# A two-branch attention kernel: state accumulated chunk by chunk in PSUM, weights resident early, four-head score groups, TensorE in written order

## The chip, the cores and the metric

The kernel runs on one core of one Trainium2 chip. The metric is the device time of one execution in microseconds (us), and lower is better. The kernel before took 442.96 us, the median of six executions (442.25 to 444.06). Every later comparison is against runs of the kernel before on the same chip in the same session; there its median lay between 443.7 and 447.4 us.

## The reference, cut to what matters

The input `x` has 2048 rows of 640 features. Two branches of 32 heads with 20 features each are computed from it and mixed with a gate for each row.

```python
def _A_ref(x, wqkv, w_phi, wo):                 # branch A: linear attention, not causal
    q, k, v = ...                               # [B, H, S, 20] from x @ wqkv
    pq, pk = q @ w_phi, k @ w_phi               # a 20x20 matrix for each head
    phi_q = concat([softmax(pq), softmax(-pq)])
    phi_k = concat([softmax(pk), softmax(-pk)])
    kv = einsum('bhsf,bhsd->bhfd', phi_k, v)    # the key-value state, over all rows
    z  = einsum('bhsf->bhf', phi_k)
    num = einsum('bhqf,bhfd->bhqd', phi_q, kv)
    den = einsum('bhqf,bhf->bhq', phi_q, z) + 1e-6
    return (num / den).reshape(B, S, D) @ wo

def _B_ref(x, wq, wk, wv, wo, beta):            # branch B: four segments of 512 rows
    phi = lambda t: where(t > 0, t + 1.0, exp(t))
    for s in range(4):
        p = softmax(qs @ ks.T * scale + mask)   # causal within the segment
        a_dot = p @ vs
        a_mem = (phi(qs) @ M) / (phi(qs) @ z + 1e-6)   # memory of earlier segments
        outs.append(g * a_mem + (1 - g) * a_dot)       # g = sigmoid(beta), one per head
        M = M + phi(ks).T @ vs
        z = z + sum(phi(ks))
    return concat(outs) @ wo

g = sigmoid((x * gate_w).sum(-1))
return g * _A_ref(x, ...) + (1 - g) * _B_ref(x, ...)
```

Of the kernel before, what the change touches and what calls it, by code (L numbers as in the profile page):

```python
# [8 lines left out]
ALU = mybir.AluOpType  # L9
# [6 lines left out]
def kernel(  # L16
# [36 lines left out]

    const = ctx.enter_context(tc.tile_pool(name="const", bufs=1))
    psw = ctx.enter_context(tc.tile_pool(name="psw", bufs=4, space=PSUM))
    pst = ctx.enter_context(tc.tile_pool(name="pst", bufs=2, space=PSUM))
# [6 lines left out]
    def stile(name):  # L63
        return pst.tile([P, 2, 512], F32, name=name, tag="st")

    xT = const.tile([P, KC, S], BF16, name="xT")
    apool_stack = ExitStack()
    apool = apool_stack.enter_context(tc.tile_pool(name="apool", bufs=1, side="right"))
    a0_stack = ExitStack()
    a0 = a0_stack.enter_context(tc.tile_pool(name="a0", bufs=1, side="right"))  # L70

    xv = x2.rearrange("(c p) d -> p c d", p=P)
    x_nat = a0.tile([P, NCH, D], BF16, name="x_nat")
    wnat_k = a0.tile([P, KC, D], BF16, name="wnat_k")
    wnat_q = a0.tile([P, KC, D], BF16, name="wnat_q")
    Wc = a0.tile([P, NG6, DH], BF16, name="Wc")
    WvA = apool.tile([P, KC, D + 1], BF16, name="WvA")
    nc.sync.dma_start(out=x_nat[:, 0:4, :], in_=xv[:, 0:4, :])
    nc.scalar.dma_start(out=wnat_k, in_=A_wqkv[:, D:2 * D].rearrange("(c p) n -> p c n", p=P))
    nc.sync.dma_start(out=WvA[:, :, 0:D],  # L80
                      in_=A_wqkv[:, 2 * D:3 * D].rearrange("(c p) n -> p c n", p=P))
    wphi_rows = A_w_phi.rearrange("h f g -> (h f) g")
    nc.gpsimd.memset(Wc[:, NG6 - 1, :], 0.0)
# [3 lines left out]
    nc.sync.dma_start(out=WvA[:, :, D:D + 1],  # L87
                      in_=gate_w.rearrange("(c p o) -> p c o", p=P, o=1))
    beta_b = const.tile([P, H], BF16, name="beta_b")
    nc.scalar.dma_start(out=beta_b, in_=B_beta.partition_broadcast(P))  # L90
    nc.sync.dma_start(out=x_nat[:, 4:8, :], in_=xv[:, 4:8, :])
    nc.scalar.dma_start(out=x_nat[:, 8:12, :], in_=xv[:, 8:12, :])
    nc.sync.dma_start(out=x_nat[:, 12:16, :], in_=xv[:, 12:16, :])
    nc.scalar.dma_start(out=wnat_q, in_=A_wqkv[:, 0:D].rearrange("(c p) n -> p c n", p=P))
# [9 lines left out]
    def block_mask(name, n, step, width, parts):  # L104
# [10 lines left out]
    chk4 = block_mask("chk4", 4, 32, 32, P)  # L115
    ind = const.tile([P, 4], BF16, name="ind")
    nc.vector.tensor_copy(out=ind, in_=chk4)

    Wphi = a0.tile([P, NG6, 6, DH], BF16, name="Wphi")
    nc.vector.tensor_tensor(out=Wphi[0:120],  # L120
                            in0=Wc[0:120, :, None, :].to_broadcast([120, NG6, 6, DH]),
                            in1=m6[0:120, None, :, None].to_broadcast([120, NG6, 6, DH]),
                            op=ALU.mult)
# [3 lines left out]

    def fold_weight(wn, dst, nm):
        WT = a0.tile([P, NG6, KC, P], BF16, name=f"WT{nm}")
        for g in range(NG6):  # L130
            gw = GW[g]
            tp = wtile("wtp", BF16)
            for ic in range(KC):
                nc.tensor.transpose(out=tp[0:gw, ic * P:(ic + 1) * P],
                                    in_=wn[:, ic, g * 120:g * 120 + gw], identity=ident_b)
            if g % 2 == 0:
                nc.scalar.copy(out=WT[0:gw, g], in_=tp[0:gw, 0:D].rearrange("p (c k) -> p c k", k=P))
            else:
                nc.vector.tensor_copy(out=WT[0:gw, g],
                                      in_=tp[0:gw, 0:D].rearrange("p (c k) -> p c k", k=P))  # L140
        for ic in range(KC):
            for (g0, g1) in ((0, 4), (4, 6)):
                ps = wtile("wfold")
                for g in range(g0, g1):
                    gw = GW[g]
                    o = (g - g0) * 120
                    nc.tensor.matmul(ps[:, o:o + gw], lhsT=WT[0:gw, g, ic, :],
                                     rhs=Wphi[0:gw, g].rearrange("p h f -> p (h f)")[:, 0:gw],
                                     start=True, stop=True)
                w = sum(GW[g0:g1])  # L150
                if g0 == 0:
                    nc.scalar.copy(out=dst[:, ic, 0:w], in_=ps[:, 0:w])
                else:
                    nc.vector.tensor_copy(out=dst[:, ic, 480:480 + w], in_=ps[:, 0:w])

    def x_transpose(sc):
        tp = wtile("xtp", BF16)
        for c in range(KC):
            nc.tensor.transpose(out=tp[:, c * P:(c + 1) * P], in_=x_nat[:, sc, c * P:(c + 1) * P],
                                identity=ident_b)  # L160
        nc.vector.tensor_copy(out=xT[:, :, sc * P:(sc + 1) * P],
                              in_=tp[:, 0:D].rearrange("p (c k) -> p c k", k=P))

    EkN = apool.tile([P, NCH, EKW], BF16, name="EkN")
    nc.gpsimd.memset(EkN[:, :, 1280:EKW], 0.0)
    vA = apool.tile([P, NCH, D], BF16, name="vA")
    gl = const.tile([P, NCH], F32, name="gl")
    KVZ = const.tile([P, 2, NG6, 6, 22], BF16, name="KVZ")
    nc.vector.tensor_copy(
        out=KVZ[:, :, :, :, DH].rearrange("p s g h -> p (s g) h"),  # L170
        in_=m6[:, None, :].to_broadcast([P, 2 * NG6, 6]))
    zc = apool.tile([P, 2 * NG6, 64], BF16, name="zc")
    zh = apool.tile([P, 2 * NG6, 2], BF16, name="zh")
    zf = apool.tile([P, 2 * NG6], BF16, name="zf")

    with tc.tile_pool(name="a1w", bufs=3, side="right") as a1w:
        def mm_x(ps, sc, W, lo, hi):
            for c in range(KC):
                nc.tensor.matmul(ps, lhsT=xT[:, c, sc * P:(sc + 1) * P], rhs=W[:, c, lo:hi],  # L179
                                 start=(c == 0), stop=(c == KC - 1))  # L180

        def a1_v(sc):
            for hf in range(2):
                ps = wtile("va_ps")
                w = 320 + hf
                mm_x(ps[:, 0:w], sc, WvA, 320 * hf, 320 * hf + w)
                nc.scalar.copy(out=vA[:, sc, 320 * hf:320 * hf + 320], in_=ps[:, 0:320])
                if hf:
                    nc.vector.tensor_copy(out=gl[:, sc:sc + 1], in_=ps[:, 320:321])

        def a1_k(sc):
            ps = stile("ka_ps")
            for hf in range(2):
                mm_x(ps[:, hf, 0:320], sc, WkA, 320 * hf, 320 * hf + 320)
            Ek = a1w.tile([P, 2, D], BF16, name="Ek")
            for sgn in range(2):
                nc.scalar.activation(out=Ek[:, sgn].rearrange("p (t f) -> p t f", t=2),  # L197
                                     in_=ps[:, :, 0:320], func=ACT.Exp,
                                     scale=1.0 if sgn == 0 else -1.0)
            ksum = a1w.tile([P, 2 * H], F32, name="ksum")  # L200
            krec = a1w.tile([P, 2 * H], F32, name="krec")
            for sgn in range(2):
                nc.vector.tensor_reduce(out=ksum[:, sgn * H:(sgn + 1) * H],  # L203
                                        in_=Ek[:, sgn].rearrange("p (h f) -> p h f", f=DH),
                                        axis=AX.X, op=ALU.add)
            nc.vector.reciprocal(out=krec, in_=ksum)  # L206
            nc.gpsimd.tensor_tensor(  # L207
                out=EkN[:, sc, 0:1280].rearrange("p (h f) -> p h f", f=DH),
                in0=Ek.rearrange("p s (h f) -> p (s h) f", f=DH),
                in1=krec[:, :, None].to_broadcast([P, 2 * H, DH]), op=ALU.mult)  # L210

        for sc in range(4):
            x_transpose(sc)
        fold_weight(wnat_k, WkA, "k")
        for sc in range(NCH):
            a1_v(sc)
            a1_k(sc)
            if sc + 4 < NCH:
                x_transpose(sc + 4)
        fold_weight(wnat_q, WqA, "q")  # L220
    a0_stack.close()

    gS = const.tile([P, NCH], F32, name="gS")
    omgS = const.tile([P, NCH], F32, name="omgS")
    nc.scalar.activation(out=gS, in_=gl, func=ACT.Exp, scale=-1.0)
    nc.vector.tensor_scalar_add(out=gS, in0=gS, scalar1=1.0)
    nc.vector.reciprocal(out=gS, in_=gS)
# [325 lines left out]
    for u in fill_bkv(0):  # L553
        u()
# [98 lines left out]
```

## The kernel before: the parts that the change touches

The kernel has three stages. The first part projects keys and values of branch A and builds its state. Attention then walks through 4 segments times 8 groups of four heads. A tail writes out the last segment.

In the first part, all 16 chunks of rows are projected first. The state follows as twelve passes over all chunks. A GpSimd chain sums `zh`, and only then are the weights of branch B loaded.

```python
    for sgn in range(2):
        for g in range(NG6):
            ps = wtile("kv_ps")
            for sc in range(NCH):
                lhsT = EkN[:, sc, sgn * D + g * 120:sgn * D + g * 120 + P]
                nc.tensor.matmul(ps[:, 0:gw], lhsT=lhsT, rhs=vA[:, sc, g * 120:g * 120 + gw],
                                 start=(sc == 0), stop=(sc == NCH - 1), ...)
                nc.tensor.matmul(ps[:, 128 + 4 * sc:132 + 4 * sc], lhsT=lhsT, rhs=ind, ...)
            ...
    for j in range(1, 32):
        nc.gpsimd.tensor_tensor(out=zh, in0=zh, in1=zcv[:, :, :, j], op=ALU.add)
    ...                                         # only now: weights of branch B
    nc.sync.dma_start(out=WkB, in_=B_wk...)     # and WvB, WoA, WoB
    for c in range(KC):
        nc.sync.dma_start(out=wq_st, in_=B_wq[c * P:(c + 1) * P, :])
        nc.gpsimd.tensor_copy(out=WqB[:, c, :, 0:DH], in_=wq_st...)
```

PSUM holds four work buffers (`wtile`) and two score buffers (`stile`) of twice that size. Almost everything in attention takes a work buffer and gives it back when the last reader has finished:

```python
    def wtile(name, dt=F32):                    # psw has bufs=4
        return psw.tile([P, 512], F32, name=name, tag="w")
    def stile(name):                            # pst has bufs=2
        return pst.tile([P, 2, 512], F32, name=name, tag="st")

    def b_q(s, g):                              # query projection of a group
        ps = wtile("qb_ps")
        ...                                     # 5 matmuls of 512 columns
        nc.vector.tensor_copy(out=qT, in_=ps)
        if s > 0:
            nc.scalar.activation(out=eq, in_=ps, func=ACT.Exp)    # second reader of ps
            ...

    def b_v(s, c):                              # value projection of a chunk
        for hf in range(2):
            ps = wtile("vb_ps")
            mm_x2(ps[:, 0:320], 4 * s + c, WvB, ...)
            nc.scalar.copy(out=vb[...], in_=ps[:, 0:320]...)

    def b_qk(qT, kT, PTs, cs):                  # scores, one pair of heads at a time
        for pr in range(2):
            st = stile("st_ps")
            for c in cs:
                for i in range(2):
                    nc.tensor.matmul(st[:, i, o:o + n], ..., tile_position=(64 * pr + 32 * i, 0))
            nc.scalar.activation(out=PTs[pr]..., in_=st[:, :, 0:w], func=ACT.Exp, scale=SCALE_B)

    def a3_num(s, qc, half):                    # a "num unit": output of branch A, 1/8 of a segment
        for sgn in range(2):
            ps = wtile("num_ps")                # two work buffers
            ...                                 # 3 matmuls
            nc.scalar.copy(out=dz[...], in_=v[:, :, DH:DH + 2])
        ...                                     # VectorE: xx, rr, 1/rr, cs (four small steps)
        for sgn in range(2):                    # only this frees the two buffers
            nc.vector.tensor_tensor(out=ts[:, sgn, ...], in0=pss[sgn][:, :, 0:DH],
                                    in1=cs[...], op=ALU.mult)
```

Beside the groups' own work, each segment has "filler" units in a queue: key and value projections of the next segment (`kb`, `vb`), the `pq` and `num` units of branch A, and the output projection of the segment before. The loop emits a share of them after each third of a group. The first query projection of the next segment comes after everything else:

```python
            mix = []                            # a3 = 6 pq units, then 8 num units
            while fins or a3:
                if a3: mix.append(a3.pop(0))
                if fins: mix.append(fins.pop(0))
            for t in range(max(nm, nr)):        # rest = kb, vb of the next segment
                if t < nr: queue.append(rest[t])
                if t < nm: queue.append(mix[t])
        for t, cs in enumerate(((0,), (1, 3), (2,))):
            b_qk(qT, kT, PTs, cs)
            ...                                 # next group's b_q, b_kT, unless a new segment
            want = (ntot * sl) // nslots
            while done < want:
                queue[done]()
                done += 1
        if k + 1 < NG and (k + 1) % G == 0:     # new segment: query comes last
            nxt = (b_q(s1, g1), b_kT(s1, g1))
```

The order in the code is not the order on TensorE. In the kernel before, a scheduler reorders the instructions of every engine when the program is built, and may put a later, independent matmul ahead of a waiting one.

The softmax here doesn't subtract the row's maximum and nothing guards it: scores larger than these inputs give would overflow.

## Time and profile before

| | before |
|---|---|
| median (first six executions) | 442.96 us |
| profiled span | 443.1 us |
| first query projection (`qb`) starts | 121.9 us |
| attention (to the end of the last value matmul) | 301.6 us |
| tail | 19.6 us |

The first view gives windows of the profile of the kernel before, one for each stage and one for the end of a segment. The columns are the window and its length in us, then the busy time of TensorE (PE), its weight load, VectorE (DVE), ScalarE (ACT) and GpSimd (POOL), each with a count of instructions. Then come the granted TensorE clock, the share of DMA and GB/s.

```profile
core 0: us, PE busy (x) PEld busy (x) DVE busy (x) ACT busy (x) POOL busy (x), PEclk, DMA share, GB/s
0.00:23.40 23.40, 9.70 (x86) 8.28 (x87) 6.57 (x19) 6.13 (x10) 3.47 (x18) 1.00 0.93 297
23.40:121.90 98.50, 81.33 (x900) 63.51 (x899) 58.19 (x117) 45.32 (x101) 58.47 (x64) 0.88 0.08 24
121.90:423.50 301.60, 278.85 (x3184) 161.82 (x3182) 195.12 (x582) 224.65 (x394) 150.65 (x319) 0.93 0.02 8
423.50:443.10 19.60, 14.31 (x128) 9.94 (x124) 4.72 (x12) 3.41 (x8) 0.86 (x1) 1.00 0.12 43
180.00:190.00 10.00, 7.07 (x73) 3.96 (x72) 8.78 (x27) 3.63 (x9) 5.19 (x11) 0.56 0.01 2
```

In attention TensorE is busy for 278.9 of 301.6 us, so it is idle for only 22.8. No other engine comes near it over the whole stage. The last row shows why an average is not enough. In these 10 us, around the end of the first segment, VectorE is at 88%, ScalarE has hardly anything to do, and TensorE's clock averages 0.56.

The second view is the list of TensorE's waits over the whole kernel before, with the total in us, the number of waits and the longest.

```profile
engine line waited for: us in total, times, longest us
PE vb_ps L312 <- ACT ek L326: 12.3, 1, 12.3
...
```

The 12.3 us wait is the one between the first part and attention. The `ek` step was itself held up by the late `WqB` copies on GpSimd (12.7 us of ScalarE's idle time before `ek` ended on them).

The third view gives groups of TensorE instructions in attention: busy us, mean ns of one, then the idle time just before them and what ended it.

```profile
L383 PE MATMUL st_ps<-qT,kT 32*128 32x384 bf16 (+3 forms) x512 | 64.0, 312 | 9.2 <-ACT PT_5667 L388 0.8 <-ACT PT_4163 L388 0.8 <-ACT PT_3949 L388 0.6
...
L475 PE MATMUL num_ps<-KVZ,Eq 128*128 128x132 bf16 (+1 forms) x192 | 21.2, 230 | 4.5 <-DVE ts L495 1.4 <-DVE td L435 1.3 <-DVE kT L369 0.6
```

Another view is TensorE's timeline in the kernel before, where the second segment begins. Each line has start and length in us, the line of code, what was written and read, how many, and in brackets the idle time before and what ended it.

```profile
185.94 2.31 PE L347 MATMUL qb_ps<-xT,WqB 128*128 128x512 bf16 x5 [0.85 <-DVE ts L495]
...
190.59 0.40 PE L383 MATMUL st_ps<-qT,kT 32*128 32x512 bf16 x4
```

The first query projection of the segment waits for a work buffer that `ts` frees, and the segment's first scores follow 4.7 us later. This is one of the bubbles that the change sets out to remove.

### The profile page before, as it was taken

What the parts mean: (1) busy time and instruction counts of PE and PEld (TensorE: products, weight loads), DVE (VectorE), ACT (ScalarE), POOL (GpSimd) and SP (SyncE); (2) the same over time, 40 slices, a digit from 0 to 9 for tenths busy, and PEclk for the clock granted to TensorE, in tenths of its full rate; (3) what the DMA queues carried; (4) which work ended last, traced back from release to release, by engine and by line L of the source; (5) the groups of instructions that cost most, each with busy time, mean ns of one, the idle gap of its engine ahead of it and who ended that gap; (6) DMA issues with size and microseconds to landing.
All of it is one profiled execution on the core that took longest, in us unless ns stands there. A gap on an engine that the chain in (4) does not pass through costs nothing.

```text
span 443.1 us, 10565 instructions
## 1 busy us (share of the span) xinstructions
PE 384.2 (87%) x4288; PEld 243.6 (55%) x4288; DVE 264.6 (60%) x728; ACT 279.5 (63%) x511; POOL 213.4 (48%) x402
## 2 busy tenths in 40 slices
PE   2599996991799999789998979999989899989996
PEld 2477775890545554446554555555555546555564
DVE  0468989321453467866547887444588764587731
ACT  1266675210479987477786665876774699785711
POOL 3037776817234547634335554443455645565710
PEclk9999999696799999599998899999898999896899
DMA  7950000000100000000000000000000000000001
GB/s 246 341 201 1 3 0 1 2 3 15 31 0 2 2 1 1 2 1 2 0 17 1 16 17 16 1 1 1 18 16 1 31 1 17 1 17 1 16 31 44
DMA packets 11240, 12.49 MB, mean 28 GB/s; under 512 B 1977, under 2 KB 11193, under 8 KB 11193
## 3 DMA queue, kind: packets, MB, share of 16 engines
q1 hardware_dynamic: 9209, 9.53, 6.6%
q10 hardware_dynamic: 1984, 2.30, 1.5%
q8 instruction: 33, 0.54, 0.5%
q14 instruction: 14, 0.11, 0.1%
HBM read 9.21 MB, written 2.62 MB: 27 GB/s over the span
## 4 chain that ended last, share of the span: by engine, by line
PE 58%; DVE 15%; ACT 14%; issue 5%; POOL 4%; DMA 3%; POOLq 0%; DVEq 0%; ACTq 0%
PE o_ps L525 8%; PE st_ps L383 7%; PE qb_ps L347 6%; PE nd_ps L402 5%; PE pq_ps L457 5%; PE ka_ps L179 4%; PE va_ps L179 4%; PE vb_ps L312 4%; PE kv_ps L250 3%; PE kb_ps L312 3%; DMA Wc<-in_A_w_phi_dram 3%; DVE ts L495 2%; PE num_ps L475 2%; DVE xx L484 2%; POOL zh L262 2%
## 5 line engine op out<-in xcount | busy, mean ns | idle before, releaser
L383 PE MATMUL st_ps<-qT,kT 32*128 32x384 bf16 (+3 forms) x512 | 64.0, 312 | 9.2 <-ACT PT_5667 L388 0.8
L207 POOL TENSOR_TENSOR EkN<-Ek,krec 128x1280 bf16<-128x1280 bf16 x16 | 37.7, 2355 | 36.4 <-DVE krec L206 36.0
L347 PE MATMUL qb_ps<-xT,WqB 128*128 128x512 bf16 x160 | 44.8, 410 | 1.7 <-DVE ts L495 1.6
L312 PEld LDWEIGHTS <-xT 128*128 128x128 bf16 x320 | 30.6, 100 | 28.5 <-issue 16.0
L383 PEld LDWEIGHTS <-kT 32*128 32x128 bf16 x512 | 19.1, 92 | 38.5 <-issue 28.4
L529 ACT CAST osb<-o_ps 128x320 bf16<-128x320 f32 x32 | 13.7, 429 | 40.4 <-PE o_ps L525 40.3
L351 DVE CAST qT<-qb_ps 128x512 bf16<-128x512 f32 x32 | 22.0, 688 | 27.3 <-PE qb_ps L347 27.2
L179 PEld LDWEIGHTS <-xT 128*128 128x128 bf16 x320 | 30.7, 98 | 11.4
L312 PE MATMUL vb_ps<-WvB,xT 128*128 128x320 bf16 x160 | 25.8, 310 | 12.3 <-ACT ek L326 12.3
L500 POOL TENSOR_TENSOR oA<-ts 128x360 bf16<-128x360 f32 (+1 forms) x32 | 27.5, 860 | 18.3 <-DVE ts L495 17.1
L431 DVE RECIPROCAL rd<-nd_ps 128x16 f32<-128x16 f32 x32 | 8.1, 253 | 46.0 <-PE nd_ps L402 45.9
L457 PE MATMUL pq_ps<-xT,WqA 128*128 128x512 bf16 x120 | 30.1, 379 | 0.3 <-DVE kT L369 0.2
L495 DVE TENSOR_TENSOR ts<-num_ps,cs 128x360 f32<-128x360 f32 (+1 forms) x64 | 28.4, 484 | 2.0
L197 ACT ACTIVATE Ek<-ka_ps 128x640 bf16<-128x640 f32 x32 | 20.8, 701 | 13.9 <-PE ka_ps L179 13.0
L203 DVE TENSOR_REDUCE ksum<-Ek 128x32 f32<-128x640 bf16 x32 | 24.7, 814 | 2.1 <-ACT Ek L197 1.8
L347 PEld LDWEIGHTS <-WqB 128*128 128x128 bf16 x160 | 14.1, 102 | 21.6 <-issue 9.1
L312 PE MATMUL kb_ps<-WkB,xT 128*128 128x320 bf16 x160 | 25.4, 303 | 0.3 <-DVE kT L369 0.3
L445 POOL TENSOR_TENSOR oB<-td,tm 128x320 bf16<-128x320 f32 x24 | 20.6, 859 | 10.5 <-DVE td L435 10.1
L475 PE MATMUL num_ps<-KVZ,Eq 128*128 128x132 bf16 (+1 forms) x192 | 21.2, 230 | 4.5 <-DVE ts L495 1.4
L179 PE MATMUL ka_ps<-WkA,xT 128*128 128x320 bf16 x160 | 24.9, 299 | 0.0
L179 PE MATMUL va_ps<-WvA,xT 128*128 128x320 bf16 (+1 forms) x160 | 24.5, 300 | 0.0
L326 ACT ACTIVATE ek<-kb_ps 128x320 bf16<-128x320 f32 x24 | 10.1, 443 | 19.7 <-POOL WqB L307 12.7
(470 smaller groups left out, 1018.6 us busy)
## 6 DMA issues: line engine op xcount, KB each, us to landing
out_dram<-osb SPq DMA_DIRECT2D x16, 160.0 KB, 1.8
x_nat<-in_A_x_dram SPq DMA_DIRECT2D x3, 640.0 KB, 7.6
wnat_k<-in_A_wqkv_dram ACTq DMA_DIRECT2D x1, 800.0 KB, 7.8
WvA<-in_A_wqkv_dram SPq DMA_DIRECT2D x1, 800.0 KB, 10.6
wnat_q<-in_A_wqkv_dram ACTq DMA_DIRECT2D x1, 800.0 KB, 13.3
WkB<-in_B_wk_dram SPq DMA_DIRECT2D x1, 800.0 KB, 9.5
WvB<-in_B_wv_dram SPq DMA_DIRECT2D x1, 800.0 KB, 10.4
WoA<-in_A_wo_dram SPq DMA_DIRECT2D x1, 800.0 KB, 10.9
```

Source lines behind the costliest of these rows:

```text
L179: nc.tensor.matmul(ps, lhsT=xT[:, c, sc * P:(sc + 1) * P], rhs=W[:, c, lo:hi], start=(c == 0), stop=(c == KC - 1))
L203: nc.vector.tensor_reduce(out=ksum[:, sgn * H:(sgn + 1) * H], in_=Ek[:, sgn].rearrange("p (h f) -> p h f", f=DH), axis=AX.X, op=ALU.add)
L207: nc.gpsimd.tensor_tensor(out=EkN[:, sc, 0:1280].rearrange("p (h f) -> p h f", f=DH), in0=Ek.rearrange("p s (h f) -> p (s h) f", f=DH), in ...
L312: nc.tensor.matmul(ps, lhsT=xT[:, c, sc * P:(sc + 1) * P], rhs=W[:, c, lo:hi], start=(c == 0), stop=(c == KC - 1))
L347: nc.tensor.matmul(ps, lhsT=WqB[:, c, 4 * g:4 * g + 4, :], rhs=xT[:, c, s * L:(s + 1) * L], start=(c == 0), stop=(c == KC - 1))
L383: nc.tensor.matmul(st[:, i, o:o + n], lhsT=kT[r:r + 32, c * P:(c + 1) * P], rhs=qT[r:r + 32, c * P:L], start=True, stop=True, tile_positio ...
L402: nc.tensor.matmul(nd[:, j * 84 + i * V1:j * 84 + (i + 1) * V1], lhsT=PTs[i // 2][:, i % 2, o:o + P], rhs=vb[:, c, 4 * g + i, :], start=(j ...
L457: nc.tensor.matmul(ps, lhsT=WqA[:, c, g * 120:g * 120 + P], rhs=xT[:, c, s * L:(s + 1) * L], start=(c == 0), stop=(c == KC - 1))
L475: nc.tensor.matmul(ps[:, o:o + GH[g] * 22], lhsT=segs[s].Eq[g][:, sgn, qc * P:(qc + 1) * P], rhs=KVZ[:, sgn, g, 0:GH[g], :].rearrange("p h ...
L495: nc.vector.tensor_tensor(out=ts[:, sgn, 0:nh, :], in0=pss[sgn][:, :, 0:DH], in1=cs[:, sgn, 0:nh, None].to_broadcast([P, nh, DH]), op=ALU. ...
L500: nc.gpsimd.tensor_tensor(out=segs[s].oA[:, qc, h0 * DH:(h0 + nh) * DH].rearrange("p (h d) -> p h d", d=DH), in0=ts[:, 0, 0:nh, :], in1=ts ...
L525: nc.tensor.matmul(ps[:, 0:320], lhsT=segs[s].oT[X][:, k5 * P:(k5 + 1) * P], rhs=Wo[:, k5, hf * 320:hf * 320 + 320], start=(n == 0), stop= ...
```

## The change

The change has five intents.

1. Small loads go first, and all weights of branch B are loaded at the start and kept.
2. The state is accumulated in PSUM after each chunk, between the projections, and not in passes at the end. The `WqB` copies go to VectorE.
3. The score matmuls of all four heads of a group are issued together. The 24 value copies of attention go from ScalarE to VectorE (the copies of the first segment's values move too).
4. The filler units are dealt by an estimated TensorE time for each, beginning with projections. The next segment's first query is issued a group ahead.
5. TensorE keeps the written order (`manual_schedule`); the other engines are still reordered.

The core of the diff (cuts marked with "..."; remarks after `#` are added here):

```diff
+    ctx.enter_context(tc.manual_schedule(engines={mybir.EngineType.PE}))
...                                             # loads: small ones first, all weights here
+    wload(WkB, B_wk)
+    wload(WvB, B_wv)
...
+    nc.gpsimd.memset(WqB[:, :, :, DH:32], 0.0) # fills of branch B's buffers, now at the start
+        nc.gpsimd.memset(kp[:, :, :, DH:32], 0.0)
+        nc.gpsimd.memset(pk[:, :, :, DH:32], 0.0)
...
+    def a1_kv(sc):                             # state matmuls of one chunk
+        for idx in (0, 1, 2, 3, 4, 6, 7, 8, 9, 10, 5, 11):
+            nc.tensor.matmul(acc[bank][:, o:o + gw], lhsT=lhsT,
+                             rhs=chunk[sc].v[:, g * 120:g * 120 + gw],
+                             start=(sc == 0 and o == 0), stop=(sc == NCH - 1), ...)
...
+    for sc in range(NCH):
+        if sc + 2 < NCH:
+            a1_v(sc + 2)
+        a1_k(sc)
...
+        if sc >= 2:
+            a1_kv(sc - 2)
+    for c in range(KC):
+        nc.vector.tensor_copy(out=WqB[:, c, :, 0:DH], ...)
-    for sgn in range(2):                       # the twelve passes of the state
-        for g in range(NG6):
...
-            nc.scalar.copy(out=vb[:, c, hf * 16:hf * 16 + 16, 0:DH],
+            nc.vector.tensor_copy(out=vb[:, c, hf * 16:hf * 16 + 16, 0:DH],
...
     def b_qk(qT, kT, PTs, cs):
+        st2 = [pst.tile([P, 2, 512], F32, name="st_ps", tag="st") for _ in range(2)]
+        for c in cs:
+            for i in range(4):
+                nc.tensor.matmul(st2[i // 2][:, i % 2, o:o + n], ..., tile_position=(32 * i, 0))
...
+            base = deal(fill_bkv(s + 1) if s + 1 < NSEG else [], fill_a3(s))
+            head = []
+            while base and sum(t for t, _ in head) < total / G - own + 0.5:
+                head.append(base.pop(0))
+            queue = head + deal(base, fins)
...
             if t == 0 and k + 1 < NG:
-                s1, g1 = divmod(k + 1, G)
-                if not (g1 == 0):
-                    nxt = (b_q(s1, g1), b_kT(s1, g1))
+                nq = b_q(*divmod(k + 1, G))    # the next segment's first query too
...
-        if k + 1 < NG and (k + 1) % G == 0:
-            nxt = (b_q(s1, g1), b_kT(s1, g1))
```

The `deal` order is worked out in the code, so it can be read off. In the two middle segments, the number of `num` units in each of the eight groups was 0 0 0 0 2 2 3 1 before, and is 0 0 0 0 0 2 2 4 after.

## The prediction

> **What bounds it now.** The windows view splits the 442.96 us into four stages.
> 1. 0 to 23 us, loading. TensorE is busy 9.7 us; the chain of waits begins with the 23 KB load `Wc`, 12.5 us to landing behind large loads.
> 2. 23 to 122 us, first part. Projections are TensorE-dense until 69.5. Then the query fold (69.5 to 80.4, 6.0 us busy), 384 state matmuls (16 us), and about 13 us idle: the waits view has TensorE 12.3 us behind ScalarE `ek`, which waits for GpSimd's `WqB` copies, queued behind its 32-step `zh` chain and late weight loads.
> 3. 122 to 423.5 us, attention. Busy: TensorE 279, ScalarE 225, VectorE 195, GpSimd 151 of 301.5. At full-clock spacing (216 ns for 512 columns, 136 for 320, 25 for 21) TensorE needs about 225. Limits alternate: VectorE is 84 to 90% busy at segment ends, where the `num` units bunch, and ScalarE is then starved (3.6 of 10 us in 180 to 190), because the next segment's first query projection comes last.
> 4. 423.5 to 443, output tail.
>
> The clock records hold about 65 us at exactly half clock, in multiples of 3.41 us, 41 of them in attention. [...]
>
> **What the change does on the critical path.**
> - Loading: small loads first, gate weights as a row plus one transpose. Steady projections begin near 17 instead of 23: -6.
> - State chunk by chunk: the same 384 matmuls (78 ns a pair, 0.94 us a chunk), between projections. Per chunk TensorE needs about 4.2 us against ScalarE 2.9, VectorE 2.8, GpSimd 3.4 (2.36 for `EkN`, four adds of 0.24): still TensorE-bound. The fold's bubbles go: -5.
> - Weights early, `WqB` on VectorE, no `zh` tail: -13. Given back: about 4, as VectorE waits for `wq_st` and ScalarE for `beta_b`, landing at 20 to 36 us.
> - So attention begins near 96 instead of 122.
> - Attention: same work, except 24 value copies (10 us) moving from ScalarE to VectorE. Laying the written unit order over traced durations, the busiest engine of each group sums to about 257 us after, 252 before: `num` units bunch even more tightly into a segment's last quarter. No gain from balance. The gain is the next segment's first query issued a group ahead, removing three boundary bubbles (4 to 6 each), and less half clock: 301 becomes about 280.
> - Four-head score groups: four 512-column score matmuls already took 0.33 us when issued together[...]. Only split pairs gain: under 4, mostly off the path.
> - Tail unchanged, 19 to 20.
>
> **Prediction: 96 + 280 + 19 = 395 us**, 80% range 374 to 415. Faster by over 2%: 0.95; within 2%: 0.04; slower: 0.01.
>
> **What would show it.** First `qb` matmul at 90 to 102; no TensorE wait over 4 us after 20 us; state matmuls spread over 25 to 90 us; mean granted clock at least 0.95; VectorE busy about 205 us in attention, over 85% in a segment's last two groups; ScalarE without the boundary dips; attention lasting 265 to 297.
>
> **What would make it wrong.** Written order leaves TensorE standing where the scheduler had other work: score matmuls now need both score buffers free, and `num` units hold buffers while VectorE is behind. Then attention stays at 300, the total near 415. Or VectorE keeps up better than its traced durations suggest: attention 260, total 375. Early loads could starve `x` and delay the first part.

Two of the numbers can be set against the traces. Four 512-column score matmuls issued together took 0.39 to 0.40 us in the kernel before, not 0.33. "20 to 36 us" was an estimate; in the kernel after VectorE's copies of `wq_st` start between 27.7 and 35.3 us, and `beta_b` is read at 35.5.

## The result, and the profile after

The kernel after took 439.75 us (median of 20 runs, 438.17 to 444.61), against 443.72 us for 40 runs of the kernel before. The ratio of fast runs is 0.992, with a 95% interval of 0.989 to 0.994. It is the same within 2%, far from the predicted 395. A ratio here is the mean time of one kernel's fast runs over that of the other's fast runs of the same rounds, so it is not quite the ratio of the medians quoted. Executions over 1.5% slower than the fastest of the same kernel are left out of the means.

| stage | before | predicted | after | change |
|---|---|---|---|---|
| loading and first part | 121.9 | 96 | 98.9 | -23.0 |
| attention | 301.6 | 280 | 316.6 | +15.0 |
| tail | 19.6 | 19 | 22.3 | +2.7 |
| profiled span | 443.1 | 395 | 437.8 | -5.3 |

The windows of the kernel after, cut as before at the first query projection and at the end of attention:

```profile
0.00:21.90 21.90, 11.88 (x101) 8.91 (x101) 10.37 (x19) 7.00 (x13) 11.17 (x26) 1.00 0.95 309
21.90:98.90 77.00, 74.16 (x885) 57.94 (x886) 57.29 (x105) 45.84 (x128) 54.76 (x84) 1.00 0.11 33
98.90:415.50 316.60, 265.12 (x3187) 155.87 (x3185) 206.38 (x608) 217.69 (x369) 149.24 (x318) 0.92 0.02 8
415.50:437.80 22.30, 16.52 (x126) 10.96 (x122) 4.79 (x13) 3.41 (x8) 1.74 (x3) 0.85 0.09 30
250.00:260.00 10.00, 5.54 (x38) 2.69 (x35) 9.36 (x25) 3.98 (x11) 5.04 (x9) 0.76 0.06 19
```

The first part did what it was meant to do: between 21.9 and 98.9 us TensorE is busy for 74.2 of 77.0 us at full clock. Attention gave most of that back. TensorE's busy time there fell by 13.7 us, but its idle time rose from 22.8 to 51.5. The last row is again the end of a segment, this time the second. VectorE is at 94%, TensorE at 55%, and ScalarE is starved just as before.

The groups of TensorE instructions in attention, after:

```profile
L426 PE MATMUL st_ps<-qT,kT 32*128 32x128 bf16 (+3 forms) x512 | 44.4, 315 | 12.0 <-ACT PT_2021 L434 0.9 <-ACT PT_2287 L434 0.9 <-DVE kT L413 0.9
...
L518 PE MATMUL num_ps<-KVZ,Eq 128*128 128x132 bf16 (+1 forms) x192 | 19.1, 226 | 16.7 <-DVE ts L538 8.4 <-DVE td L481 2.5 <-ACT eq L399 2.0
```

The idle time before `num` went from 4.5 to 16.7 us, half of it behind `ts`, the VectorE step that frees a `num` unit's two work buffers.

The list of TensorE's waits in attention, after:

```profile
PE num_ps L518 <- DVE ts L538: 8.4, 7, 1.8
PE mz_ps L465 <- DVE ts L538: 3.8, 4, 1.0
...
PE vb_ps L231 <- ACT eq L399: 2.4, 4, 0.8
PE kT_ps L410 <- DVE ts L538: 2.2, 2, 1.2
```

Most of these waits end on two releasers: `ts` on VectorE, and `eq` on ScalarE. The latter is the second reader of a query projection's work buffer. Neither of the two is an input of `mz` or `kT`. What those matmuls need from them is the buffer.

The following timeline shows TensorE in the kernel after at the end of the second segment, with the columns as above. Its first line is the third segment's first query projection, now a group ahead.

```profile
241.81 1.25 PE L391 MATMUL qb_ps<-xT,WqB 128*128 128x512 bf16 x5
...
249.76 0.62 PE L518 MATMUL num_ps<-KVZ,Eq 128*128 128x132 bf16 x9
251.23 0.35 PE L518 MATMUL num_ps<-KVZ,Eq 128*128 128x132 bf16 x3 [0.85 <-DVE td L481]
253.34 0.67 PE L518 MATMUL num_ps<-KVZ,Eq 128*128 128x132 bf16 x6 [1.77 <-DVE ts L538]
253.94 0.39 PE L426 MATMUL st_ps<-qT,kT 32*128 32x512 bf16 x4
255.27 2.31 PE L391 MATMUL qb_ps<-xT,WqB 128*128 128x512 bf16 x5 [0.93 <-DVE ts L538]
...
258.73 0.46 PE L465 MATMUL mz_ps<-vB_158,phik_157 128*128 128x84 bf16 x4 [0.86 <-DVE ts L538]
```

And VectorE in the same stretch of the kernel after:

```profile
252.84 0.81 DVE L538 TENSOR_TENSOR ts<-num_ps,cs 128x280 f32<-128x280 f32 x2
...
254.68 0.97 DVE L538 TENSOR_TENSOR ts<-num_ps,cs 128x360 f32<-128x360 f32 x2
...
258.23 0.79 DVE L538 TENSOR_TENSOR ts<-num_ps,cs 128x280 f32<-128x280 f32 x2
```

Read the two together. The `num` matmuls belong to three units in a row (six matmuls each), and each unit takes two of the four work buffers. VectorE's records show 2.6 to 3.5 us for the chain of one unit, from `xx` to `ts`. So the third unit waits for the first unit's `ts` (253.34, in the course of the one from 252.84). The third segment's first scores (253.94) stand behind it, though their query had been projected by 243.06. Then the query projection of that segment's second group waits for the second unit's `ts` (255.27), and behind it `mz` waits for the third unit's (258.73). In this stretch no matmul overtakes a waiting one: the scores start 0.6 us after the wait of 1.77 us has ended. The query projection then takes 2.31 us for five matmuls, because half clock has set in (granted clock 0.50 from 255.3 to 262.1). At full clock (241.81) the same five take 1.25 us.

The following table is worked out from the starts of the groups' first score matmuls. It sums groups 6 and 7 of a segment and group 0 of the next, over the three boundaries:

| | groups 6, 7 and next 0, three boundaries |
|---|---|
| before | 94.1 us |
| after | 108.3 us |

The difference, 14.2 us, is nearly all of attention's +15.0. So the net loss sits at the ends of the segments. The runs below split this. With the units in the order of before (e1) the sum is 95.0 us, but with TensorE free and the units still dealt (e2) it stays at 109.1. What the free order gains in e2 lies in the other groups: up to the last group's first scores they take 183.8 us there, against 193.4 in the kernel after and 195.1 in the kernel before.

### The profile page after: what moved, and what is told of

The parts are those of the page before. It is cut to its first block, busy times and chain, and to the rows that moved or that the text cites. A ratio compares the mean times of both kernels' runs of the same rounds, so it can differ in the third digit from the quotient of the medians.

```text
span 437.8 us, 10636 instructions
## 1 busy us (share of the span) xinstructions
PE 367.7 (84%) x4289; PEld 233.7 (53%) x4289; DVE 278.8 (64%) x743; ACT 273.9 (63%) x515; POOL 216.9 (50%) x430
## 4 chain that ended last, share of the span: by engine, by line
PE 56%; DVE 18%; ACT 16%; issue 5%; POOL 3%; DMA 2%; SPq 0%; POOLq 0%; DVEq 0%; ACTq 0%
PE o_ps L568 11%; PE qb_ps L391 6%; PE st_ps L426 5%; PE nd_ps L448 5%; PE vb_ps L231 5%; PE pq_ps L500 4%; PE va_ps L231 4%; PE kb_ps L231 4%; DVE ts L538 3%; PE ka_ps L231 3%; DVE rr L529 2%; ACT eq L399 2%; DVE xx L527 2%; DVE qT L395 2%; PE kT_ps L410 1%
## 5 line engine op out<-in xcount | busy, mean ns | idle before, releaser
L426 PE MATMUL st_ps<-qT,kT 32*128 32x128 bf16 (+3 forms) x512 | 44.4, 315 | 12.0 <-ACT PT_2021 L434 0.9
L391 PE MATMUL qb_ps<-xT,WqB 128*128 128x512 bf16 x160 | 46.1, 425 | 1.9 <-DVE ts L538 1.9
L395 DVE CAST qT<-qb_ps 128x512 bf16<-128x512 f32 x32 | 22.1, 690 | 36.5 <-PE qb_ps L391 36.3
L572 ACT CAST osb<-o_ps 128x320 bf16<-128x320 f32 x32 | 13.7, 427 | 37.2 <-PE o_ps L568 37.1
L426 PEld LDWEIGHTS <-kT 32*128 32x128 bf16 x512 | 14.2, 92 | 40.9 <-issue 35.4
L518 PE MATMUL num_ps<-KVZ,Eq 128*128 128x132 bf16 (+1 forms) x192 | 19.1, 226 | 16.7 <-DVE ts L538 8.4
L231 PE MATMUL kb_ps<-WkB,xT 128*128 128x320 bf16 x160 | 27.2, 315 | 3.2 <-ACT eq L399 1.6
L241 ACT CAST vA<-va_ps 128x320 bf16<-128x320 f32 x32 | 13.7, 427 | 22.4 <-PE va_ps L231 22.4
L251 ACT ACTIVATE Ek<-ka_ps 128x320 bf16<-128x320 f32 x64 | 23.0, 439 | 5.5 <-PE ka_ps L231 4.8
L518 PEld LDWEIGHTS <-Eq 128*128 128x128 bf16 x192 | 13.1, 102 | 21.3 <-DVE ts L538 11.3
L256 DVE TENSOR_REDUCE ksum<-Ek 128x64 f32<-128x1280 bf16 x16 | 23.7, 1481 | 0.7
L399 ACT ACTIVATE eq<-qb_ps 128x512 bf16<-128x512 f32 x24 | 14.6, 609 | 11.8 <-DVE qT L395 11.6
## 6 DMA issues: line engine op xcount, KB each, us to landing
WoA<-in_A_wo_dram SPq DMA_DIRECT2D x1, 800.0 KB, 10.4
```

The costliest lines, as they stand in the source:

```text
L231: nc.tensor.matmul(ps, lhsT=xT[:, c, sc * P:(sc + 1) * P], rhs=W[:, c, lo:hi], start=(c == 0), stop=(c == KC - 1))
L251: nc.scalar.activation(out=Ek[:, sgn, 320 * hf:320 * hf + 320], in_=ps[:, 0:320], func=ACT.Exp, scale=1.0 if sgn == 0 else -1.0)
L256: nc.vector.tensor_reduce(out=ksum, in_=Ek.rearrange("p s (h f) -> p (s h) f", f=DH), axis=AX.X, op=ALU.add)
L391: nc.tensor.matmul(ps, lhsT=WqB[:, c, 4 * g:4 * g + 4, :], rhs=xT[:, c, s * L:(s + 1) * L], start=(c == 0), stop=(c == KC - 1))
L426: nc.tensor.matmul(st2[i // 2][:, i % 2, o:o + n], lhsT=kT[r:r + 32, c * P:(c + 1) * P], rhs=qT[r:r + 32, c * P:L], start=True, stop=True, ...
L518: nc.tensor.matmul(ps[:, o:o + GH[g] * 22], lhsT=segs[s].Eq[g][:, sgn, qc * P:(qc + 1) * P], rhs=KVZ[:, sgn, g, 0:GH[g], :].rearrange("p h ...
```

## The experiments

Five theories were tried. The expectations name them by letter.

- **A**: the bunched `num` units put VectorE behind and hold the work buffers. This hurts only because TensorE may not overtake.
- **B**: the written order of TensorE costs by itself, whatever the order of units.
- **C**: the four-head score groups cost, since both score buffers must be free at once.
- **D**: in the first microseconds VectorE is held up while GpSimd fills buffers.
- **E**: there are too few PSUM work buffers, and the query's buffer is held too long by its second reader `eq`.

All kernels gave correct results. Diffs are against the kernel after, cut to their core, except for one that starts from the kernel before. Medians are given with the ratio to the kernel before and its 95% interval.

### The unit order of before (e1)

```diff
-            base = deal(fill_bkv(s + 1) if s + 1 < NSEG else [], fill_a3(s))
-            ...
-            queue = head + deal(base, fins)
+            ...                       # mix and rest, interleaved as in the kernel before
-            while queue and (spent + 0.5 * queue[0][0] < due or (g == G - 1 and t == 2)):
+            while done < (ntot * (3 * g + t + 1)) // (3 * G):
```

> The changed kernel with one thing undone: the filler units of each segment (projections, num, output) are queued in the order of the kernel before, by count, instead of dealt by estimated TensorE time. Theory A (num units bunched into a segment's last quarter put VectorE behind; the matmul work buffers stay full and TensorE, in written order, stands): attention falls from 317 us to about 300, total near 424, TensorE time around num matmuls falls from 34 to about 22 us, and VectorE is less dense in the last two groups. Theory B (written order as such costs, whatever the units' order): total stays at 437 to 442. Theory C (four-head score groups cost): stays too.

Measured: 423.26 us, ratio 0.954 (0.949 to 0.959), attention 302.5 us. The dealt order alone costs 16 us. Attention is still not faster than before.

### TensorE free (e2)

```diff
-    ctx.enter_context(tc.manual_schedule(engines={mybir.EngineType.PE}))
```

> The changed kernel without the written order on TensorE: the scheduler may reorder its instructions again; nothing else is changed. Theory B: total falls by 12 to 18 us, to near 424, as attention goes back to about 300. Theory A: the same bunched num units meet the same VectorE, so at most half of that comes back, 432 to 440. If the scheduler reorders badly it may be slower than 440, and then written order was a gain.

Measured: 427.27 us, ratio 0.964 (0.958 to 0.969), attention 308.5 us. The total is nearer to B's forecast than to A's, but attention did not come back to 300. The written order also costs, 12 us with the dealt units. Taking away the line lets the build choose TensorE's order, and the other engines' orders shift a little with it. So this is "written against scheduled", not TensorE's order alone.

### Value copies back on ScalarE (e3)

```diff
-            nc.vector.tensor_copy(out=vb[:, c, hf * 16:hf * 16 + 16, 0:DH],
+            nc.scalar.copy(out=vb[:, c, hf * 16:hf * 16 + 16, 0:DH],
```

> The changed kernel with the second part's value copies (32 copies of 128x320, about 0.41 us of VectorE each) put back on ScalarE. Theory A: VectorE is what limits at segment ends, and one or two value units fall there, so 3 to 7 us are saved, total 433 to 437. Theories B and C: under 2 us either way, since ScalarE has room.

Measured: 438.95 us, ratio 0.990 (0.984 to 0.995), attention 316.3 us. Nothing changed. The gain that A expected was missed. A likely reason, not tested, is that the copies come with the projections and not in the stretches where VectorE is late.

### Scores in pairs again (e4)

```diff
     def b_qk(qT, kT, PTs, cs):
-        st2 = [pst.tile(...) for _ in range(2)]      # four heads, both buffers
+        for pr in range(2):
+            st = pst.tile([P, 2, 512], F32, name="st_ps", tag="st")
+            ...                                      # two heads, one buffer
```

> The changed kernel with score matmuls issued pair by pair as before: a pair needs only one score buffer, and the exponential of the first pair need not wait for the second buffer. Theory C (needing both buffers at once stops TensorE and ScalarE about 0.4 us three times a group): total falls by 10 us or more, to under 430. Theory A or B: the total rises by 3 to 10 us, since score matmuls took 65.5 us of TensorE's time in attention before and 50.9 after.

Measured: 439.65 us, ratio 0.993 (0.986 to 1.000), attention 315.8 us. C falls: the four-head groups neither cost nor gain. In the profile of this run the score matmuls are busy for 44.9 us, as against 44.4 in the kernel after and 64.0 before. So even the lower busy time of the scores does not come from grouping them in fours. The loss that A and B expected is missed too. (The expectation's 65.5 and 50.9 us are not the busy times of these lists.)

### Num units spread over the segment (e5)

```diff
-        u = [(1.08, lambda g=g: a3_pq(s, g)) for g in range(NG6)]
-        for qc in range(4):
-            u += [(0.37, ... a3_num(s, qc, 0)), (0.37, ... a3_num(s, qc, 1))]
+        pq = [(1.08, lambda g=g: a3_pq(s, g)) for g in range(NG6)]
+        n0, n1 = [[(1.6, lambda qc=qc, h=h: a3_num(s, qc, h)) for qc in range(4)] for h in range(2)]
+        return pq[0:3] + [n0[0], pq[3], n0[1], pq[4], n0[2], pq[5], n0[3]] + n1
```

The `num` units of the first half need only the first three `pq` units, so they can start early. With the weight of 1.6 the counts in the middle segments become 0 1 1 1 1 1 1 2.

> The changed kernel, written order kept; only the order of units within a segment is new: the four num units of the first half may follow after three of the six query features, and num counts 1.6 instead of 0.37 when units are dealt, so that its 2 us of VectorE are spread over the segment. Theory A (bunching on VectorE is what costs): groups 6, 7 and the next 0, now 12 to 14 us, fall to 9 to 11; attention is at most 300 and the total at most 424, perhaps 415. Theory B (written order itself costs 12 us): the total stays above 430.

Measured: 426.97 us (424.28 to 431.05), ratio 0.958 (0.941 to 0.974). The runs scatter, and the profiled one was slow; the three fast ones have a median of 425.50 us. So the size is rough, and the verdict at 2% is unclear, but all four are faster than every run of the kernel after.

### Unit order of before and TensorE free (e6)

The edits of e1 and e2 together.

> The changed kernel with both undone: the units in the order of the kernel before, and TensorE free for the scheduler. If bunched units and written order only cost together (A: written order is harmless where VectorE keeps up), the total equals that of the units alone, 420 to 426. If written order costs by itself (B), another 8 to 12 us come off: 411 to 415.

Measured: 417.91 us, ratio 0.939 (0.929 to 0.949), attention 297.5 us. This run says most about the early query. Order of units and freedom of TensorE are those of before, but the next segment's first query comes a group ahead. The sum over the three boundaries is 93.6 us, against 94.1 before. The total lies between what A and B expected. A segment's last group became shorter (first boundary 16.2 to 9.4 us), and the next segment's first group became longer by nearly as much (7.8 to 13.5). The bubble moved; it did not go away. The early query was not tried on the kernel before alone, and the value copies and four-head groups differ here too. But e3 and e4 found those two neutral under the written order.

### Buffer fills on VectorE (e7)

```diff
-    nc.gpsimd.memset(WqA[:, :, D:728], 0.0)
-    nc.gpsimd.memset(WqB[:, :, :, DH:32], 0.0)
+    nc.vector.memset(WqA[:, :, D:728], 0.0)
+    nc.vector.memset(WqB[:, :, :, DH:32], 0.0)
...                                   # and kpad, phik, vB, Msb
```

> The changed kernel with the fills of the second part's tiles (10 us on GpSimd while loading) moved to VectorE. In the profile three VectorE instructions of about 0.5 us last 5.7 us each and end when GpSimd's fills end, at 11.6 us, and TensorE waits 5.2 us for them. Theory D (VectorE is held while GpSimd fills): no VectorE instruction above 1.5 us there, the first query projection moves from 98.9 to 93 to 96, total down by 3 to 6 us. Rival (VectorE waits for data that land then): nothing moves, or it gets later by the 5 us of fills.

Measured: 439.85 us, ratio 0.988 (0.978 to 0.998), attention 316.8 us. The wait that it aims at is seen in the head of the kernel after. First VectorE in the kernel after:

```profile
5.05 0.91 DVE L166 TENSOR_TENSOR Wphi<-Wc,m_128 120x720 bf16<-120x720 bf16 x1 [3.15 <-DMA Wc<-in_A_w_phi_dram]
5.88 5.68 DVE L135 CAST ind<-bd_132 128x4 bf16<-128x4 f32 x1
...
6.05 5.68 DVE L213 COPY xT<-xtp 128x640 bf16<-128x640 bf16 x2
```

Then GpSimd in the same stretch of the kernel after:

```profile
5.80 1.37 POOL L153 MEMSET phik_151<- 128x1536 bf16 x1
7.12 0.66 POOL L154 MEMSET vB_152<- 128x128 bf16 x1
...
10.57 0.97 POOL L159 MEMSET Msb<- 128x672 f32 x1
```

A cast of 128x4 elements takes 5.68 us and ends as the last fill ends, at 11.56. TensorE waits 5.2 us for the `xT` copy, held up in the same stretch. In e7 the cast takes 0.16 us, and the copies look like this on VectorE:

```profile
8.23 0.91 DVE L213 COPY xT<-xtp 128x640 bf16<-128x640 bf16 x2
```

The stall of D is shown: with the fills gone from GpSimd it is gone (TensorE's wait for `xT` falls from 5.2 to 1.5 us), and the first value projection starts at 9.29 us where it was 12.29. How the fills hold VectorE is not shown. As a cost it is nothing. The first query projection starts at 99.6 us, no earlier than 98.9. The traces show where the 3 us go. By the starts of the projections, e7 is 3.0 us ahead until about 25 us and 0.9 us ahead from about 38 us. In between, VectorE's `WqB` copies wait 2.2 us for the loads of `wq_st` (1.3 in the kernel after), which is a likely part of it. The rest goes in a stretch of 3.4 us at half clock from 85.3 us, which the kernel after does not have; behind it e7 is 0.7 us late. (The mean clock of the profiled run is 0.934, against 0.938 in the kernel after.) Why the clock fell there is not shown.

### The kernel before with TensorE in written order (e8)

This one is the kernel before with one line added.

```diff
+    ctx.enter_context(tc.manual_schedule(engines={mybir.EngineType.PE}))
```

> The kernel before with TensorE in written order and nothing else changed. Theory A (written order harmless with these less bunched units): within 2% of the kernel before, 438 to 450. Theory B: slower by 10 us or more, over 453.

Measured: 453.23 us (449.36 to 457.89), ratio 1.022 (1.003 to 1.041), attention 305.5 us. The runs scatter, and the verdict at 2% is unclear. One of the four is slow (457.89); the three fast ones average 451.9 us, against 445.9 for the three fast runs of the kernel before in that session, which is a ratio of 1.014. So the written order probably costs some us in a kernel that has nothing else of the change, but less than the 10 that B expected. TensorE's waits in attention rise from 20.4 to 41.7 us.

### Query buffer given back earlier (e10)

`eq` reads the copy `qT` instead of PSUM. The work buffer is then free after VectorE's copy. The arithmetic differs a little (`qT` is rounded to 16 bits); the result stays correct.

```diff
-            nc.scalar.activation(out=eq, in_=ps, func=ACT.Exp)
+            nc.scalar.activation(out=eq, in_=qT, func=ACT.Exp)
```

> The changed kernel with one edit: the exponential of the second part's query reads the copy qT in SBUF instead of the PSUM tile, so that VectorE's copy alone frees that work buffer. Theory E (the four work buffers are what written order trips over: the waits of TensorE put down to this exponential sum to about 8 us): total falls by 5 to 10 us, to 430 to 435, and no TensorE wait names eq. Rival (VectorE alone limits): the waits move to ts and the total falls under 2 us.

Measured: 434.73 us, ratio 0.978 (0.975 to 0.980), attention 312.7 us. TensorE's waits for `eq` in attention, 7.7 us in all in the kernel after, are gone, and 5.0 us of time with them. E is real, and small.

### The same with the unit order of before (e11), and with TensorE free as well (e12)

The edits of e1 and e10, and those of e1, e2 and e10.

> The same edit on top of the units in the order of the kernel before (which alone gave about 423): E expects 415 to 419, the rival 421 to 425.

> The same edit with the units in the order of the kernel before and TensorE left to the scheduler (418 without the edit). A scheduler that fills waits has less to gain from an earlier buffer: 413 to 417 by E, 416 to 420 by the rival. Candidate for the best version.

Measured: e11 421.76 us, ratio 0.949 (0.946 to 0.952); e12 407.06 us, ratio 0.915 (0.912 to 0.918), attention 288.0 us. The free order is worth 15 us here, though the units are no longer dealt. So the part of A that says the written order is harmless with better-placed units falls, and B stands. E's 415 to 419 for e11 was missed: 421.76 is what its rival expected, and hardly differs from e1.

### Spread units, TensorE free, early buffer (e13), and its parts (e14 to e16)

e13 is e2, e5 and e10 together. e14 leaves out e10, e15 leaves out e2, and e16 leaves out e5.

> The same edit with the num units spread over the segment and TensorE left to the scheduler. If spreading VectorE's work is worth more than the order of the kernel before, under 413; if what matters is only that num units aren't in the last quarter, 413 to 420.

> Spread num units, TensorE free, the exponential reading PSUM as in the change. With the version that has all three at 398: if the early buffer is worth its 11 us of the units-before pair (418 to 407), this is 407 to 411. If written order is the main cost, this is at most 402.

> Spread num units and the early buffer, but TensorE in written order. If written order costs by itself even where neither VectorE nor buffers press (theory B): 410 or more, against 398. If it only costs where they do (theory A): 398 to 404.

> The units as the change deals them, TensorE free, the early buffer. If bunching costs by itself even for a free TensorE: 412 to 422. If it only costs in written order: 398 to 405.

Measured, with the others of the grid (medians of the fast runs in us, since e5 and e14 have one slow run each; written or free order of TensorE, late or early release of the query buffer):

| order of the filler units | written, late | written, early | free, late | free, early |
|---|---|---|---|---|
| dealt | 439.75 (after) | 434.73 (e10) | 427.27 (e2) | 419.81 (e16) |
| as before | 423.26 (e1) | 421.76 (e11) | 417.91 (e6) | 407.06 (e12) |
| spread | 425.50 (e5) | 420.43 (e15) | 401.32 (e14) | **398.32 (e13)** |

e13 has a ratio of 0.894 (0.889 to 0.900) to the kernel before. e14 has 0.903 (0.897 to 0.908), e15 0.944 (0.940 to 0.949), e16 0.944 (0.939 to 0.949). Along the rows, freeing TensorE gains 12 and 15 us with dealt units, 5 and 15 with the order of before, 24 and 22 with spread units. Down the columns, spreading the dealt units gains 14, 14, 26 and 21 us. The early buffer gains 1.5 to 11 us. Two cells are noisy (e5 and e6), and the grid mixes sessions and chips: the kernel before had a median of 447.4 us in the session of e5 and e6, and of 443.7 to 445.0 in the others. So single differences are good to some us only. Undoing the dealt order and freeing TensorE each count in every pairing that was tried. Spreading beats the order of before only where TensorE is free (by 17 and 9 us; in written order by -2 and 1). The early buffer counts in most; its 1.5 us between e1 and e11 are within the scatter of the runs, and the 3 us between e14 and e13 are hardly more.

The windows of e13, its attention and its tail:

```profile
98.50:378.60 280.10, 265.10 (x3172) 156.09 (x3170) 201.28 (x609) 215.31 (x369) 148.91 (x318) 0.97 0.03 9
378.60:398.40 19.80, 14.64 (x138) 10.14 (x135) 4.69 (x12) 3.41 (x8) 1.72 (x2) 0.98 0.10 34
```

TensorE's busy time in attention, 265.1 us, is that of the kernel after to the hundredth of a per cent, yet attention takes 280 us and not 317. Almost all of the difference is idle time, 15.0 us against 51.5. (The last value matmuls of e13 end at 379.2, so this cut is 0.6 us early; for the kernels before and after it is within 0.2.)

Part of why a written order costs even with spread units is seen in the instructions. Timeline of TensorE in e15, written order, in the second half of a group:

```profile
124.17 0.28 PE L426 MATMUL st_ps<-qT,kT 32*128 32x256 bf16 x2 [0.40 <-ACT PT L434]
125.09 0.28 PE L426 MATMUL st_ps<-qT,kT 32*128 32x256 bf16 x2 [0.63 <-ACT PT L434]
125.30 0.58 PE L448 MATMUL nd_ps<-vB,PT 128*128 128x21 bf16 x16
```

And the same kind of place in e13, where TensorE is free:

```profile
128.97 0.28 PE L425 MATMUL st_ps<-qT,kT 32*128 32x256 bf16 x2 [0.47 <-ACT PT L433]
129.18 0.57 PE L447 MATMUL nd_ps<-vB,PT 128*128 128x21 bf16 x16
129.60 0.43 PE L230 MATMUL kb_ps<-WkB,xT 128*128 128x320 bf16 x2
129.97 0.28 PE L425 MATMUL st_ps<-qT,kT 32*128 32x256 bf16 x2
```

In e13 the projection `kb` is cut up and put between the halves of the score groups, in the time in which the second score buffer is not yet free. In e15 nothing comes between the halves, and TensorE stands at the second one (125.09, idle for 0.63 us, with `nd` behind it). Over the kernel, the waits of TensorE for the score buffers (ScalarE's `PT`) are 9.2 us in 21 waits in e15 and 4.5 us in 11 in e13. That is a part only: all waits in attention are 33.9 us in e15 and 12.8 in e13, and those for `ts` are 11.0 and 3.7. The boundaries hardly differ (83.8 us in e15, 82.3 in e13); the other groups take 202.6 and 183.7.

The following table gives TensorE's waits in attention by releaser, summed from the lists of waits:

| us | before | after | e1 | e2 | e10 | e13 |
|---|---|---|---|---|---|---|
| VectorE `ts` (holds `num` buffers) | 7.7 | 23.2 | 13.4 | 9.6 | 22.1 | 3.7 |
| ScalarE `eq` (holds the query buffer) | 0 | 7.7 | 7.8 | 3.8 | 0 | 0 |
| ScalarE `PT` (holds score buffers) | 8.4 | 10.4 | 8.0 | 11.2 | 10.4 | 4.5 |
| all waits | 20.4 | 49.9 | 36.1 | 29.5 | 44.4 | 12.8 |

### The best version with the fills on VectorE (e17)

e13 and e7 together.

> The version with all three (398), with the fills on VectorE, which moved the first projections by 3 us but not the first query projection: 396 to 400, no gain beyond the noise, if the end of the first part is bound by GpSimd's chain; 393 to 396 if not.

Measured: 397.77 us, ratio 0.894 (0.888 to 0.899), the first query projection at 99.3 us. There is no gain over e13. e13 beats both kernels by about 10%, with the work of the kernel after.

## Why the prediction was right or wrong

**The first part: right.** Predicted was a first query projection near 96 us, within 90 to 102. It came at 98.9. TensorE's longest wait from 20 us to there was 2.2 us (predicted: none over 4). The state matmuls lay at 31 to 95 us (predicted 25 to 90). One term was off: steady projections were to begin near 17 us, and began near 22 (near 19 in e7), held up at the start in part by the stall of D. Since e7 removed most of that stall and gained nothing, the term was mis-sized but did not decide the sum. The terms of the first part were not tried one by one, so only their sum is shown.

**The failed step: "301 becomes about 280".** It rested on "the next segment's first query issued a group ahead, removing three boundary bubbles (4 to 6 each), and less half clock". This was not so, for two reasons.

- *The bubble was moved, not removed.* In e6 the three boundaries sum to 93.6 us, against 94.1 before. At the end of a segment VectorE was already 88% busy before, and the early query takes none of its work away. What one group no longer waited for, the next one did. In the kernel after itself the early query was ready 11 us before its scores (243.06 and 253.94): they stood behind the `num` units. Where these are spread, the sum falls, to 82.3 us in e13 and 83.8 in e15. Nor was there less half clock in attention: 47.8 us after, 41.0 before.
- *A cost was missing from the sum.* Attention took 316.6 us, so the step missed by 36.6. The grid shows what the missing cost consists of. The dealt order of `num` units, the written order of TensorE, and the query buffer held by `eq` together make up the 41 us between the kernel after and e13, and each counts alone (14, 12 and 5 us, with the other two left as they are). The combined 41 is more than the 32 that these add up to: spreading and freeing are worth more together. That e13's attention comes to the predicted 280 does not confirm the step, since e13 has three edits that the prediction did not have.

**A sum of work is no schedule.** The prediction laid the units over durations and found 257 us of load of the busiest engine after, 252 before, and concluded "no gain from balance". As a count of work that held: VectorE's busy time in attention was 206 us (predicted about 205). Over 85% in a segment's last two groups was predicted, and came only in part: in the second and third segments it was 90 and 88% in the seventh group, and 73% in the last. But the prediction took the bunching, which it had seen, as neutral. With four buffers, and two taken by each unit, three units in a row turned VectorE's lag into idle time of TensorE. The idle time before `num` rose from 4.5 to 16.7 us.

**Its own warning came true.** "Written order leaves TensorE standing", "`num` units hold buffers while VectorE is behind", "then attention stays at 300, the total near 415". That was the mechanism, at nearly twice the size: 37 us over the predicted 280, not 20. The part of the warning about both score buffers did not come true (e4). A result not faster by 2%, as it came, had been given a chance of 0.05.

**The value copies: harmless, as predicted.** 10 us more on VectorE cost nothing (e3). **The four-head groups: neutral** (e4), near the prediction's "under 4, mostly off the path".

**Half clock.** A mean clock of at least 0.95 was predicted; it was 0.94 in the profile of after (0.93 before) and 0.98 in e13. Attention has 47.8 us at half clock after, 41.0 before, 17.1 in e13 (where the clock over attention averages 0.97). The order of the three is that of TensorE's idle time (51.5, 22.8 and 15.0 us), so the half clock may be a part of each of the three costs. But the two do not always go together: e8 has twice the waits of the kernel before (41.7 against 20.4 us) and 37.5 us at half clock (mean clock of its profiled run 0.931, against 0.927 before). The half clock was not tried on its own, and what sets it off is not shown. In the 3.4 us ahead of a stretch TensorE was busy for 0.95 to 2.02 us in the attention of the kernel after, but for 2.68 to 3.01 in that of the kernel before. The stretches in both lasted 3.4, 6.8 or 13.7 us. The tail's 22.3 us against 19.6 fits a part for the clock: it was 0.85 there, where e13's tail with 0.98 took 19.8.

**ScalarE's dips at the boundaries** were to go and did not: 3.98 of 10 us busy at the end of the second segment. The query did come earlier, on TensorE too (241.81 in the timeline). But the score matmuls, which feed ScalarE, stood behind three `num` units (253.94), and in written order nothing passed them.

What stays open is which share of the free order's gain comes from TensorE itself, and which from the other engines' orders that shift with it; also what the half clock adds, and what the early query does alone.

## What to carry to other kernels

Before pinning an engine to the written order, ask which buffers each instruction must wait for, and whether independent work stands directly behind it. If such work exists and a scheduler was using it, the written order can turn late releases into idle time: here freeing TensorE gained 12 us with dealt units (e2) and 22 with spread ones (e13 against e15). Place units that hold scarce buffers by the time that their slowest reader needs, not by their own time on TensorE, and spread them out: here this, with a free order and an earlier release, made the same work take 280 us instead of 317. And with a bubble at a boundary, ask whether the engine that limits the boundary gets less to do there. Here moving one instruction ahead only moved the bubble (93.6 us over both sides in e6, 94.1 before), and with VectorE's work spread and the query buffer given back early it was smaller (82.3 in e13). So compare the sum over both sides.
